# A queue written out unit by unit, global keys and values written in place, and four banks for the last outputs, in a fused attention and maxout kernel

## Chip, cores and metric

The kernel runs on one core of one Trainium2 chip. The metric is device time in microseconds (us) of one execution, as the median of several runs; before the change it is 216.99 us (216.52 to 217.34, three runs).

## What is computed

Attention over a band of 96 keys plus the first 8 keys of each batch, with a bias that falls with distance, then a feed-forward part that takes the maximum of three products:

```python
def _attn_ref(q, k, v, n_global, n_local):            # q, k, v: (4, 8, 768, 64) f32
    scores = scale * np.matmul(q, k.transpose(0, 1, 3, 2))
    rel = pos[:, None] - pos[None, :]
    is_global = pos[None, :] < 8
    is_local = (rel >= 0) & (rel < 96)
    dist = np.where(is_global & ~is_local, 96.0, np.abs(rel))
    slopes = 2.0 ** (-8.0 * (np.arange(H) + 1) / H)
    scores = scores - slopes[:, None, None] * dist
    scores = np.where(is_global | is_local, scores, -1e9)
    a = np.exp(scores - max);  a = a / (sum(a) + 1e-09)
    return np.matmul(a, v)

x = attention.transpose(0, 2, 1, 3).reshape(3072, 512)
h = np.maximum(np.maximum(x @ w1, x @ w2), x @ w3)    # w1..w3: (512, 768)
out = h @ w_out                                       # w_out: (768, 512)
```

## The kernel before

**Tiles.** The 4 batches of 768 rows are 24 tiles of 128 rows, T = 0 to 23, six to a batch. A row sees keys of its own tile, of the tile before, and the 8 global keys of its batch. So each tile has two blocks of scores, against itself and against the tile before, and the first 8 keys of the tile before are replaced by the global ones. The first tile of a batch has one block.

**Steps of a tile**, each a function. `load` issues three DMAs (q, k, v) on SP into one of 6 `raw` buffers. `cast` makes bf16 of q and k (line 115) and of v (line 117) on POOL. `u_X` (X) transposes q and k on PE, eight matmuls into the one `tp` bank, and ACT copies the result to `qkT` (line 148). `make_kg` and `make_vg` on POOL copy the transposed keys and the values to tiles of their own and put the global keys and values over the first 8 (lines 136 and 137, 125 and 126). `u_S` (S) makes the scores of four heads, and ACT their exponential (line 178); there are two groups of heads, g = 0 and 1, and one bank pair `sp`. DVE multiplies with the weights of mask and bias (M, line 182). `u_A` (A) multiplies with the values on PE; DVE divides by the sum. `u_XT` (XT) transposes the tile's result back on PE and DVE copies it to `xT`.

**Feed-forward.** Tiles are gathered to chunks of 4, 2, 2, 4, 4, 4 and 4. For chunk c, F1(c,f,j) is the product of xT with block f (0 to 5) of weight j (0 to 2): four matmuls, 512 columns wide for a chunk of four tiles and 256 for two. ACT copies j = 0, DVE takes the maximum with j = 1 and j = 2. F2(c,tt), the output of one tile, is six matmuls into the single `po` bank, a copy on ACT (line 249) and a DMA on SP. Weights come as nine DMAs, three to a group g = f // 2, and are cast by ACT, DVE and POOL (lines 273 to 275); w_out comes as three DMAs and is cast by ACT.

**Order.** No scheduler orders the instructions: each engine runs its own in the order in which the program issues them, and waits where data or a buffer is missing. The list `att` holds the attention steps; for chunk c the loop emits F1 units and the outputs of chunk c-1, and spreads the attention steps of chunk c+1 evenly between them. An M is emitted one step after its S. Casts, key and value copies and loads hang on X: X of tile T is followed by its copies, the cast of tile T+1 and the loads up to tile T+5. The three casts of a weight group go together, the first after the attention of chunk 0, the others after F1(0,0,2) and F1(0,2,2).

Of the kernel before, what the change touches and what calls it, by code (L numbers as in the profile page):

```python
# [19 lines left out]
def kernel(  # L20
# [13 lines left out]
    nc = tc.nc  # L34
# [28 lines left out]
    kg_pool = ctx.enter_context(tc.tile_pool(name="kg", bufs=3))  # L63
# [23 lines left out]
    vg_ring = [persist.tile([128, H * 65], BF16, name=f"vg{i}") for i in range(3)]  # L87
# [21 lines left out]

    def cast(T):  # L110
        b, t = divmod(T, NT)
        r = raw[T]
        qk = cast_pool.tile([128, 2, DM], BF16, name="qkb", tag="qkb")
        qb[T] = qk
        nc.gpsimd.tensor_copy(qk, r[:, 0:2].rearrange("p a h d -> p a (h d)"))  # L115
        va[T] = va_first[b % 2] if t == 0 else va_ring[T % NVA]
        nc.gpsimd.tensor_copy(heads(va[T])[:, :, 0:D], r[:, 2])  # L117

    def make_vg(T):
        b, t = divmod(T, NT)  # L120
        if t == 0:
            vg[T] = va[T]
        elif t < NT - 1:
            vg[T] = vg_ring[T % 3]
            nc.gpsimd.tensor_copy(words(vg[T]), words(va[T]))
            nc.gpsimd.tensor_copy(words(vg[T][0:NG]), words(va[b * NT][0:NG]))

    def make_kg(T):
        b, t = divmod(T, NT)
        kT = qkT[T][:, 1]  # L130
        if t == 0:
            kgT[T] = kT
            nc.gpsimd.tensor_copy(kg8[b % 2], kT[:, :, 0:NG])
        elif t < NT - 1:
            kgT[T] = kg_pool.tile([128, NP, 128], BF16, name="kgT", tag="kgT")
            nc.gpsimd.tensor_copy(words(kgT[T]), words(kT))  # L136
            nc.gpsimd.tensor_copy(kgT[T][:, :, 0:NG], kg8[b % 2])

    def u_X(T):
        if T < NSTART and T % 2:  # L140
# [8 lines left out]
        make_kg(T)  # L149
        make_vg(T)  # L150
        return []

    def u_S(T, g):
        b, t = divmod(T, NT)
        alt = T < NSTART and g == 1
# [25 lines left out]
        if t:  # L181
            return [lambda: nc.vector.tensor_mul(P, P, wmask[:, g])]  # L182
        return [lambda: nc.vector.tensor_mul(P[:, :, 0], P[:, :, 0], wmask0[:, g])]

    def u_A(T, g):
        b, t = divmod(T, NT)
        if T < NSTART and g == 1:
# [4 lines left out]
        for j2 in range(2):  # L192
            for hh in range(2):
# [5 lines left out]
                if t:  # L199
                    nc.tensor.matmul(o, P[:, i, 1], heads(vg[T - 1])[:, h], start=False, stop=True,  # L200
# [8 lines left out]
        return []  # L209

    def u_XT(T):
# [3 lines left out]
        tp = psT.tile([128, NP, 128], BF16, name="xtp", tag="tp")  # L215
# [4 lines left out]
        return []  # L220
# [4 lines left out]
    def u_F1(c, f, j):  # L225
# [15 lines left out]
        return []  # L241

    def u_F2(c, tt):
        po = psP.tile([128, DM], FP32, name="po", tag="po")
        for f in range(NF):
            nc.tensor.matmul(po, ht[c][:, f, tt * 128:(tt + 1) * 128], wo[:, f],  # L246
                             start=(f == 0), stop=(f == NF - 1))
        ost = ost_pool.tile([128, DM], FP32, name="ost", tag="ost")
        nc.scalar.copy(ost, po)  # L249
        T = chunks[c][tt]  # L250
        nc.sync.dma_start(out=out[T * 128:(T + 1) * 128, :], in_=ost)
        return []
# [5 lines left out]
    def load_w(g):  # L258
        for j in range(3):
            st = stage_pool.tile([128, 4, 256], FP32, name="wst", tag="wst")  # L260
            wst[g, j] = st
            nc.sync.dma_start(out=st, in_=wsrc[j][:, g * 256:(g + 1) * 256].rearrange(  # L262
                "(i p) f -> p i f", p=128))

    def load_wo():
        for i in range(3):
            st = stage_pool.tile([128, 2, DM], FP32, name="wst", tag="wst")
            wst["o", i] = st
            nc.sync.dma_start(out=st, in_=moe_w_out[i * 256:(i + 1) * 256, :].rearrange(
                "(i p) f -> p i f", p=128))  # L270

    def cast_w(g):
        nc.scalar.copy(w123[g][:, :, 0], wst[g, 0])
        nc.vector.tensor_copy(w123[g][:, :, 1], wst[g, 1])
        nc.gpsimd.tensor_copy(w123[g][:, :, 2], wst[g, 2])

    def cast_wo(i):
        nc.scalar.copy(wo[:, 2 * i:2 * i + 2], wst["o", i])

    with tc.manual_schedule():  # L280
# [36 lines left out]

        loads = [("T", T) for T in range(1, NSTART)] + [("w", 0), ("w", 1), ("T", NSTART),
                                                        ("w", 2), ("T", NSTART + 1), ("o",)]
        loads += [("T", T) for T in range(NSTART + 2, NTT)]  # L320
        done = [0]

        def upto(*what):
            if what[0] == "T" and what[1] >= NTT:
                return
            while what in loads[done[0]:]:
                x = loads[done[0]]
                done[0] += 1
                if x[0] == "T":
                    load(x[1])  # L330
                elif x[0] == "w":
                    load_w(x[1])
                else:
                    load_wo()


        att = []
        for i in range(NSTART):
            att.append(("X", i))
            if i >= 1:  # L340
                att += [("A", i - 1, 0), ("A", i - 1, 1)]
            att += [("S", i, 0), ("S", i, 1)]
            if i >= 1:
                att.append(("T", i - 1))
        i = NSTART - 1
        att += [("A", i, 0), ("X", i + 1), ("A", i, 1), ("S", i + 1, 0), ("T", i)]
        for i in range(NSTART, NTT + 1):
            if i < NTT and i > NSTART:
                att.append(("S", i, 0))
            if i > NSTART:  # L350
                att.append(("A", i - 1, 1))
            if i < NTT:
                att.append(("S", i, 1))
            if i + 1 < NTT:
                att.append(("X", i + 1))
            if i < NTT:
                att.append(("A", i, 0))
            if i > NSTART:
                att.append(("T", i - 1))
# [103 lines left out]
```

## Time and profile before

| | |
|---|---|
| median of 3 runs | 216.99 us |
| profiled execution | 216.65 us, its span 214.9 us |
| TensorE (PE) busy | 182.7 us, 85% |
| VectorE (DVE) busy | 121.5 us, 57% |
| ScalarE (ACT) busy | 113.0 us, 53% |
| GpSimd (POOL) busy | 66.1 us, 31% |
| read from HBM, written | 25.17 MB, 6.29 MB |

A timeline row gives the start in the span, the time an instruction took, its engine and line, and in brackets the idle time before it and what ended that. SPq is SP's queue, where DMAs are issued; an issue that takes long has waited for room in the DMA queue. A chain row names what held up the end of the program at that moment. PE's matmuls overlap, so the price of a unit is from its start to the next one's start.

### The profile page before, as it was taken

The numbers are of one execution on the slowest core, as the hardware profiler recorded it, in microseconds if no ns is written. First come the engines' busy times: TensorE is split into PE (matmuls) and PEld (weight loads), VectorE is DVE, ScalarE is ACT, GpSimd is POOL, SyncE is SP. The second block draws the span as 40 slices with busy tenths as digits, with TensorE's granted clock in tenths as the row PEclk, the third lists the DMA queues.
The fourth block names the chain that finished last, engine by engine and source line by source line (L and its number), as shares of the span: only waits on it lengthen the run. The fifth ranks groups of instructions, "written<-read, shape, count | busy, mean of one in ns | idle before, by whom it ended". The sixth has DMA issues, their size and how long they took to land.

```text
span 214.9 us, 4230 instructions
## 1 busy us (share of the span) xinstructions
PE 182.7 (85%) x1640; PEld 103.1 (48%) x1640; DVE 121.5 (57%) x266; ACT 113.0 (53%) x165; POOL 66.1 (31%) x131
## 2 busy tenths in 40 slices
PE   0446825998999999789999999999999999999962
PEld 0335622543566776466555455545544555444420
DVE  2164714576674648875876878565765666532400
ACT  5855504775765756566657635565564552233231
POOL 4654322437405047135433703135505000000000
PEclk9999999999999999999999999999999999999999
DMA  7999999999999894889547980111101111012122
GB/s 151 219 218 338 319 247 274 344 193 221 219 208 222 221 259 80 195 187 196 112 110 172 232 175 0 52 49 50 52 0 52 49 49 52 2 49 83 64 100 98
DMA packets 83924, 31.73 MB, mean 148 GB/s; under 512 B 75456, under 2 KB 80064, under 8 KB 83904
## 3 DMA queue, kind: packets, MB, share of 16 engines
q1 hardware_dynamic: 83904, 31.46, 64.1%
q8 instruction: 13, 0.21, 0.4%
q14 instruction: 7, 0.06, 0.1%
HBM read 25.17 MB, written 6.29 MB: 146 GB/s over the span
## 4 chain that ended last, share of the span: by engine, by line
PE 60%; SPq 17%; ACT 10%; DMA 4%; DVE 4%; issue 2%; POOL 1%; ACTq 0%
PE h L231 35%; PE po L246 14%; SPq L108 13%; ACT P L178 5%; DMA raw<-in_v_dram 4%; PE sp L168 4%; SPq L262 3%; DVE P L182 3%; PE xtp L218 2%; ACT qkT L148 2%; PE tp L146 2%; PE op L197 2%; ACT h L236 1%; ACT ost L249 1%; PE op L200 1%
## 5 line engine op out<-in xcount | busy, mean ns | idle before, releaser
L231 PE MATMUL h<-xT,w 128*128 128x512 bf16 (+1 forms) x504 | 110.7, 353 | 3.1 <-DVE xT L219 1.6
L231 PEld LDWEIGHTS <-w 128*128 128x128 bf16 x504 | 44.0, 98 | 35.9 <-issue 1.8
L178 ACT ACTIVATE P<-sp 128x1024 bf16<-128x1024 f32 (+1 forms) x44 | 42.1, 958 | 21.6 <-PE sp L168 21.6
L182 DVE TENSOR_TENSOR P<-P,wmask 128x1024 bf16<-128x1024 bf16 x40 | 33.6, 845 | 25.0 <-ACT P L178 24.6
L238 DVE TENSOR_TENSOR h<-h,h 128x512 bf16<-128x512 bf16 (+1 forms) x42 | 25.5, 608 | 29.0 <-PE h L231 28.4
L246 PE MATMUL po<-wo,ht 128*128 128x512 bf16 x144 | 35.0, 379 | 2.2 <-ACT ost L249 2.2
L236 ACT CAST h<-h 128x512 bf16<-128x512 f32 (+1 forms) x42 | 22.2, 528 | 22.5 <-PE h L231 22.2
L249 ACT COPY ost<-po 128x512 f32<-128x512 f32 x24 | 14.1, 586 | 37.2 <-PE po L246 34.1
L115 POOL CAST qkb<-raw 128x1024 bf16<-128x1024 f32 x24 | 24.8, 1034 | 15.7 <-DMA raw<-in_k_dram 15.7
L148 ACT COPY qkT<-tp 128x1024 bf16<-128x1024 bf16 x22 | 22.3, 1014 | 13.2 <-PE tp L146 13.2
L240 DVE TENSOR_TENSOR ht<-h,h 128x512 bf16<-128x512 bf16 (+1 forms) x42 | 25.5, 608 | 5.2 <-PE h L231 3.3
L146 PE MATMUL tp<-identb,qkb 128*128 128x128 bf16 x176 | 14.9, 234 | 13.6 <-POOL qkb L115 10.7
L136 POOL COPY kgT<-qkT 128x256 int32<-128x256 int32 x16 | 6.7, 416 | 59.7 <-ACT qkT L148 59.7
L146 PEld LDWEIGHTS <-qkb 128*128 128x128 bf16 x192 | 13.8, 108 | 19.8 <-POOL qkb L115 14.7
L246 PEld LDWEIGHTS <-ht 128*128 128x128 bf16 x144 | 13.2, 98 | 16.0 <-issue 3.0
L207 DVE TENSOR_TENSOR xb<-op,rz 128x256 bf16<-128x256 f32 x44 | 18.7, 424 | 1.5
L197 PEld LDWEIGHTS <-P 128*128 128x128 bf16 x192 | 15.0, 103 | 7.7 <-DVE xb L207 2.3
L168 PE MATMUL sp<-qkT 64*128 64x128 bf16 x204 | 14.1, 231 | 3.7 <-ACT qkT L148 2.9
L168 PEld LDWEIGHTS <-qkT 64*128 64x128 bf16 x224 | 7.6, 101 | 19.5 <-issue 15.7
L197 PE MATMUL op<-va,P 128*128 128x65 bf16 x148 | 14.6, 198 | 2.5 <-DVE xb L207 1.5
L200 PEld LDWEIGHTS <-P 128*128 128x128 bf16 x160 | 12.2, 103 | 2.4
L117 POOL CAST va<-raw 128x512 bf16<-128x512 f32 x20 | 12.7, 635 | 0.1
(52 smaller groups left out, 128.8 us busy)
## 6 DMA issues: line engine op xcount, KB each, us to landing
raw<-in_q_dram SPq DMA_DIRECT2D x24, 256.0 KB, 5.0
raw<-in_k_dram SPq DMA_DIRECT2D x24, 256.0 KB, 5.0
raw<-in_v_dram SPq DMA_DIRECT2D x24, 256.0 KB, 5.0
out_dram<-ost SPq DMA_DIRECT2D x24, 256.0 KB, 2.0
wst<-in_moe_w_dram SPq DMA_DIRECT2D x9, 512.0 KB, 6.5
wst<-in_moe_w_out_dram SPq DMA_DIRECT2D x3, 512.0 KB, 5.4
```

Source lines behind the costliest of these rows:

```text
L108: nc.sync.dma_start(out=r[:, i], in_=src[b, :, sl, :].rearrange("h s d -> s h d"))
L115: nc.gpsimd.tensor_copy(qk, r[:, 0:2].rearrange("p a h d -> p a (h d)"))
L146: nc.tensor.transpose(tp[:, a, jp], qb[T][:, a, jp * 128:(jp + 1) * 128], identb)
L148: nc.scalar.copy(qkT[T], tp)
L168: nc.tensor.matmul(sps[hh][:, j2, ds], st, qkT[T][hsl, 0, jp], start=True, stop=True, skip_group_check=True)
L178: nc.scalar.activation(P[:, :, 0:n], sp.rearrange("p a b d n -> p (a b) d n")[:, :, 0:n], AF.Exp, bias=0.0, scale=scale)
L182: return [lambda: nc.vector.tensor_mul(P, P, wmask[:, g])]
L197: nc.tensor.matmul(o, P[:, i, 0], heads(va[T])[:, h], start=True, stop=(t == 0), skip_group_check=True)
L231: nc.tensor.matmul(ps, w123[f // 2][:, dm, j, (f % 2) * 128:(f % 2) * 128 + 128], xT[c][:, dm], start=(dm == 0), stop=(dm == 3))
L238: nc.vector.tensor_max(h01s[c, f], h01s[c, f], ps)
L240: nc.vector.tensor_max(ht[c][:, f], h01s[c, f], ps)
L246: nc.tensor.matmul(po, ht[c][:, f, tt * 128:(tt + 1) * 128], wo[:, f], start=(f == 0), stop=(f == NF - 1))
```

## The change

A string, `SCHEDULE`, names every unit in the order in which it is issued; one loop calls the function of each. Letters are L load, w and o weight loads, C cast (`.0` for q and k, `.1` for v), X, S, M, A as above, T for XT, G for the global keys, V for the global values, F for F1, O for F2, W and Q casts of weights, E the last four outputs.

Beside the order, these things change. `make_kg` and `make_vg` are gone: G and V write the 8 global columns and rows into the tile itself, after its own S and A have read it, and S and A of the next tile read it there. The casts of q and k and of v are two units; for tiles 0 to 3, DVE casts q and POOL k. Each M, each weight load and each weight cast is a unit. All X use the bank `tp`, and XT of tiles 0 to 3 a bank of F1. The last four outputs have a bank each (`po`, `op`, `tp`, `sp`); two at a time get five of their six matmuls before the sixth; the copies of the last two are split between ACT and DVE.

```diff
+SCHEDULE = """
+    C0.0 X0 L1 S0.0 C1.0 M0.0 S0.1 G0 X1 C0.1 S1.0 S1.1 M0.1 L2 C2.0 X2 M1.0 C1.1 G1 M1.1 A0.0 L3 C3.0
...
+    A2.0 A2.1 M3.1 T1 G3 S4.0 w1.0 C3.1 w1.2 W0.0 L6 V2 w2.0 w2.1 C5.0 A3.0 A3.1 T2 M4.0 w2.2 L7 X5 S4.1
...
+"""
-    kg_pool = ctx.enter_context(tc.tile_pool(name="kg", bufs=3))
-    vg_ring = [persist.tile([128, H * 65], BF16, name=f"vg{i}") for i in range(3)]
-    def cast(T):
+    def cast(T, what):
         b, t = divmod(T, NT)
         r = raw[T]
+        if what == 1:
+            va[T] = va_first[b % 2] if t == 0 else va_ring[T % NVA]
+            nc.gpsimd.tensor_copy(heads(va[T])[:, :, 0:D], r[:, 2])
+            return
         qk = cast_pool.tile([128, 2, DM], BF16, name="qkb", tag="qkb")
         qb[T] = qk
-        nc.gpsimd.tensor_copy(qk, r[:, 0:2].rearrange("p a h d -> p a (h d)"))
-        va[T] = va_first[b % 2] if t == 0 else va_ring[T % NVA]
-        nc.gpsimd.tensor_copy(heads(va[T])[:, :, 0:D], r[:, 2])
-
-    def make_vg(T):
...
-            nc.gpsimd.tensor_copy(words(vg[T]), words(va[T]))
-            nc.gpsimd.tensor_copy(words(vg[T][0:NG]), words(va[b * NT][0:NG]))
-
-    def make_kg(T):
...
-            nc.gpsimd.tensor_copy(words(kgT[T]), words(kT))
-            nc.gpsimd.tensor_copy(kgT[T][:, :, 0:NG], kg8[b % 2])
+        flat = r.rearrange("p a h d -> p a (h d)")
+        if T < 4:
+            nc.vector.tensor_copy(qk[:, 0], flat[:, 0])
+            nc.gpsimd.tensor_copy(qk[:, 1], flat[:, 1])
+        else:
+            nc.gpsimd.tensor_copy(qk, flat[:, 0:2])
+
+    def put_kg(T):
+
+        b, t = divmod(T, NT)
+        kT = qkT[T][:, 1]
+        if t == 0:
+            nc.gpsimd.tensor_copy(kg8[b % 2], kT[:, :, 0:NG])
+        elif t < NT - 1:
+            nc.gpsimd.tensor_copy(kT[:, :, 0:NG], kg8[b % 2])
+
+    def put_vg(T):
+        b, t = divmod(T, NT)
+        if 0 < t < NT - 1:
+            nc.gpsimd.tensor_copy(words(va[T][0:NG]), words(va[b * NT][0:NG]))
...
-                    st = qkT[T][hsl, 1, jp] if ds == 0 else kgT[T - 1][hsl, jp]
+                    st = qkT[T][hsl, 1, jp] if ds == 0 else qkT[T - 1][hsl, 1, jp]
...
-                    nc.tensor.matmul(o, P[:, i, 1], heads(vg[T - 1])[:, h], start=False, stop=True,
+                    nc.tensor.matmul(o, P[:, i, 1], heads(va[T - 1])[:, h], start=False, stop=True,
...
+    last = NCH - 1
+    spare = ["po", "op", "tp", "sp"]
+
+    def f2_mm(c, tt, fs):
+        if (c, tt) not in pos_:
+            tag = spare[tt % 4] if c == last else "po"
+            pool = {"po": psP, "op": psO, "tp": psT, "sp": psS}[tag]
+            pos_[c, tt] = pool.tile([128, DM], FP32, name="po", tag=tag)
+        for f in fs:
+            nc.tensor.matmul(pos_[c, tt], ht[c][:, f, tt * 128:(tt + 1) * 128], wo[:, f],
+                             start=(f == 0), stop=(f == NF - 1))
+
+    def f2_out(c, tt):
+        po = pos_[c, tt]
+        T = chunks[c][tt]
+        ost = ost_pool.tile([128, DM], FP32, name="ost", tag="ost")
+        if T >= NTT - 2:
+            for i, copy in enumerate((nc.scalar.copy, nc.vector.tensor_copy)):
+                sl = slice(i * 256, (i + 1) * 256)
+                copy(ost[:, sl], po[:, sl])
+            nc.sync.dma_start(out=out[T * 128:(T + 1) * 128, :], in_=ost)
...
+    def cast_w(g, j):
+        copy = (nc.scalar.copy, nc.vector.tensor_copy, nc.gpsimd.tensor_copy)[j]
+        copy(w123[g][:, :, j], wst[g, j])
...
+    def u_E():
+        n = len(chunks[last])
+        for tt in range(0, n, 2):
+            two = range(tt, min(tt + 2, n))
+            for x in two:
+                f2_mm(last, x, range(NF - 1))
+            for x in two:
+                f2_mm(last, x, [NF - 1])
+                f2_out(last, x)
...
+        units = {"L": load, "w": load_w, "o": load_wo, "C": cast, "X": u_X, "S": u_S, "M": u_M,
+                 "A": u_A, "G": put_kg, "V": put_vg, "T": u_XT, "F": u_F1, "W": cast_w,
+                 "Q": cast_wo, "O": u_F2, "E": u_E}
+        for u in SCHEDULE.split():
+            units[u[0]](*(int(n) for n in u[1:].split(".") if n))
```

SP's queue at the start, before, from the second weight group on. `raw_220` and `raw_230` are tiles 4 and 5, `wst` the weights:

```order
L262 DMA wst_214<-in_moe_w1_dram 128x4x256
L262 DMA wst_216<-in_moe_w2_dram 128x4x256
L262 DMA wst_218<-in_moe_w3_dram 128x4x256
L108 DMA raw_220<-in_q_dram 128x8x64
L108 DMA raw_220<-in_k_dram 128x8x64
L108 DMA raw_220<-in_v_dram 128x8x64
L262 DMA wst_224<-in_moe_w1_dram 128x4x256
L262 DMA wst_226<-in_moe_w2_dram 128x4x256
L262 DMA wst_228<-in_moe_w3_dram 128x4x256
L108 DMA raw_230<-in_q_dram 128x8x64
L108 DMA raw_230<-in_k_dram 128x8x64
L108 DMA raw_230<-in_v_dram 128x8x64
```

Here tiles 0 to 3 and the first weight group are already ahead, and tiles 4 and 5 follow the second and the third group.

SP's queue at the same place, now. `raw_334` and `raw_470` are tiles 5 and 6:

```order
L142 DMA raw_334<-in_q_dram 128x8x64
L142 DMA raw_334<-in_k_dram 128x8x64
L142 DMA raw_334<-in_v_dram 128x8x64
L315 DMA wst_371<-in_moe_w1_dram 128x4x256
L315 DMA wst_373<-in_moe_w2_dram 128x4x256
L315 DMA wst_388<-in_moe_w3_dram 128x4x256
L315 DMA wst_390<-in_moe_w2_dram 128x4x256
L315 DMA wst_464<-in_moe_w1_dram 128x4x256
L315 DMA wst_467<-in_moe_w3_dram 128x4x256
L142 DMA raw_470<-in_q_dram 128x8x64
L142 DMA raw_470<-in_k_dram 128x8x64
L142 DMA raw_470<-in_v_dram 128x8x64
```

Tiles 4 and 5 now stand ahead of all weights, and tile 6 between the weights of group 1 and group 2.

POOL's queue around the first weight casts, before. `raw_230`, `raw_277` and `raw_350` are tiles 5, 6 and 7; `w123_0` and `w123_1` are weight groups:

```order
L125 COPY vg1_121<-va0_114 128x260
L126 COPY vg1_121<-vaf0_118 8x260
L115 CAST qkb_520<-raw_230 128x1024
L117 CAST va1_115<-raw_230 128x8x64
L275 CAST w123_0_125<-wst_212 128x4x256
L115 CAST qkb_597<-raw_277 128x1024
L117 CAST vaf1_119<-raw_277 128x8x64
L275 CAST w123_1_126<-wst_218 128x4x256
L133 COPY kg8_1_124<-qkT_697 128x32
L115 CAST qkb_700<-raw_350 128x1024
```

Each weight cast stands behind the casts of a whole tile, that of group 1 behind those of tile 6.

POOL's queue around the same casts, now. `raw_279`, `raw_330`, `raw_334` and `raw_470` are tiles 3, 4, 5 and 6:

```order
L149 CAST va3_114<-raw_279 128x8x64
L172 COPY va2_113<-vaf0_115 8x260
L158 CAST qkb_479<-raw_334 128x1024
L326 CAST w123_0_119<-wst_388 128x4x256
L149 CAST va0_111<-raw_330 128x8x64
L172 COPY va3_114<-vaf0_115 8x260
L167 COPY qkT_405<-kg8_0_117 128x4x8
L326 CAST w123_1_120<-wst_467 128x4x256
L158 CAST qkb_629<-raw_470 128x1024
L149 CAST va1_112<-raw_334 128x8x64
```

The cast of group 1 no longer stands behind that of tile 6, the v of a tile is cast later than its q and k, and the key and value copies stand apart from the casts of the next tile.

## Rows read from the trace of the kernel before

**Rows 1.** Timeline of POOL, casts of q and k: start, us, engine line, [idle before <-releaser].
```profile
9.01 1.04 POOL L115 CAST qkb<-raw 128x1024 bf16<-128x1024 f32 x1
...
29.68 1.04 POOL L115 CAST qkb<-raw 128x1024 bf16<-128x1024 f32 x1 [4.62 <-DMA raw<-in_k_dram]
...
37.64 1.04 POOL L115 CAST qkb<-raw 128x1024 bf16<-128x1024 f32 x1 [3.19 <-DMA raw<-in_k_dram]
...
45.31 1.04 POOL L115 CAST qkb<-raw 128x1024 bf16<-128x1024 f32 x1 [5.03 <-DMA raw<-in_k_dram]
...
49.97 1.04 POOL L115 CAST qkb<-raw 128x1024 bf16<-128x1024 f32 x1 [0.57 <-DMA raw<-in_k_dram]
```
**Rows 2.** Chain of waits, 38 to 50 us: start, us, what the end waited on.
```profile
38.79 8.79 DMA raw<-in_v_dram
...
48.26 0.99 POOL w L275
...
49.30 1.04 PE h L231 x4
```
**Rows 3.** Windows: stretch, us; busy us (instructions) of PE, PEld, DVE, ACT, POOL; PEclk, DMA, GB/s.
```profile
75.00:107.00 32.00, 28.75 (x340) 19.33 (x338) 23.32 (x55) 19.49 (x28) 13.62 (x28) 1.00 0.83 173
107.00:151.00 44.00, 43.24 (x410) 22.72 (x409) 30.06 (x63) 25.79 (x34) 15.95 (x31) 1.00 0.47 103
151.00:203.00 52.00, 52.00 (x364) 25.52 (x362) 28.28 (x55) 21.42 (x31) 5.94 (x12) 1.00 0.12 46
```
**Rows 4.** Chain of waits, the last four outputs.
```profile
203.24 1.31 PE po L246 x6
...
208.96 0.59 ACT ost L249
...
209.59 1.47 PE po L246 x6
```
**Rows 5.** Chain of waits, stretches of PE alone: start to start is a unit's price.
```profile
72.63 0.44 PE h L231 x4
73.06 0.45 PE tp L146 x8
...
106.10 0.33 PE sp L168 x8
106.43 0.97 PE h L231 x4
107.40 0.03 PE op L197
...
107.64 1.29 PE po L246 x6
...
111.79 0.22 PE xtp L218 x4
...
179.93 7.77 PE h L231 x36
```
**Rows 6.** Timeline of SP, issues of v of tiles 1 and 2.
```profile
5.00 1.18 SPq L108 DMA_DIRECT2D raw<-in_v_dram  x1
...
8.55 1.10 SPq L108 DMA_DIRECT2D raw<-in_v_dram  x1
```
**Rows 7.** Timeline of PE, first and third F1 unit.
```profile
35.75 1.86 PE L231 MATMUL h<-xT,w 128*128 128x512 bf16 x4 [1.64 <-DVE xT L219]
...
40.42 1.03 PE L231 MATMUL h<-xT,w 128*128 128x512 bf16 x4
```
**Rows 8.** Timelines of DVE and POOL, 84 to 87 us.
```profile
84.19 2.87 DVE L182 TENSOR_TENSOR P<-P,wmask 128x1024 bf16<-128x1024 bf16 x1
...
85.91 0.61 POOL L117 CAST vaf<-raw 128x512 bf16<-128x512 f32 x1
```
**Rows 9.** The line of the full multiplies: duration ns min/median/max, first and last start.
```profile
L182 DVE TENSOR_TENSOR P<-P,wmask x40: 677/691/2872, 14.0 to 176.3; 128x1024 bf16<-128x1024 bf16 x40
```
**Rows 10.** Groups by line and shape: the exponentials; busy, mean ns, idle before.
```profile
L178 ACT ACTIVATE P<-sp 128x1024 bf16<-128x1024 f32 x37 | 38.0, 1026 | 17.3 <-PE sp L168 17.2
```

More of the change, by code (lines that the diff above doesn't have):

```diff
@@ L90 @@
     wo = persist.tile([128, NF, DM], BF16, name="wo")
-    raw, qb, kb, qkT, kgT, Pt, ops, xb, rzs = {}, {}, {}, {}, {}, {}, {}, {}, {}
+    raw, qb, qkT, Pt, xb = {}, {}, {}, {}, {}
     xT = {}
-    va, vg = {}, {}
+    va = {}
     def words(ap):
@@ L148, in u_X @@
         nc.scalar.copy(qkT[T], tp)
-        make_kg(T)
-        make_vg(T)
-        return []
     def u_S(T, g):
         b, t = divmod(T, NT)
-        alt = T < NSTART and g == 1
+        alt = early(T) and g == 1
         if alt:
@@ L180, in u_S, with u_M @@
                                  AF.Exp, bias=0.0, scale=scale)
-        if t:
-            return [lambda: nc.vector.tensor_mul(P, P, wmask[:, g])]
-        return [lambda: nc.vector.tensor_mul(P[:, :, 0], P[:, :, 0], wmask0[:, g])]
+    def u_M(T, g):
+        P = Pt[T, g]
+        if T % NT:
+            nc.vector.tensor_mul(P, P, wmask[:, g])
+        else:
+            nc.vector.tensor_mul(P[:, :, 0], P[:, :, 0], wmask0[:, g])
     def u_A(T, g):
         b, t = divmod(T, NT)
-        if T < NSTART and g == 1:
+        if early(T) and g == 1:
             op = psP.tile([128, 4, 65], FP32, name="opp", tag="po")
@@ L214, in u_XT @@
             xT[c] = xT_pool.tile([128, NP, len(chunks[c]) * 128], BF16, name="xT", tag="xT")
-        tp = psT.tile([128, NP, 128], BF16, name="xtp", tag="tp")
+        where_xt = 'h2' if early(T) else 'tp'
+        pool = {'h2': psH, 'tp': psT, 'po': psP, 'op': psO}[where_xt]
+        tp = pool.tile([128, NP, 128], BF16, name="xtp", tag=where_xt)
         x = xb[T].rearrange("p h d -> p (h d)")
@@ L219, in u_XT @@
         nc.vector.tensor_copy(xT[c][:, :, i * 128:(i + 1) * 128], tp)
-        return []
     ht = {}
@@ L240, in u_F1 @@
             nc.vector.tensor_max(ht[c][:, f], h01s[c, f], ps)
-        return []
-    def u_F2(c, tt):
[L244 to L252, printed above, removed]
+    pos_ = {}
@@ new lines @@
+    last = NCH - 1
[17 more added lines that the diff above has]
+            nc.sync.dma_start(out=out[T * 128:(T + 1) * 128, :], in_=ost)
+        else:
+            nc.scalar.copy(ost, po)
+            nc.sync.dma_start(out=out[T * 128:(T + 1) * 128, :], in_=ost)
@@ L254 @@
+    def u_F2(c, tt):
+        f2_mm(c, tt, range(NF))
+        f2_out(c, tt)
     wsrc = [moe_w1, moe_w2, moe_w3]
     wst = {}
[L258 to L275, printed above, removed]
+    def load_w(g, j):
+        st = stage_pool.tile([128, 4, 256], FP32, name="wst", tag="wst")
+        wst[g, j] = st
+        nc.sync.dma_start(out=st, in_=wsrc[j][:, g * 256:(g + 1) * 256].rearrange(
+            "(i p) f -> p i f", p=128))
+    def load_wo(i):
+        st = stage_pool.tile([128, 2, DM], FP32, name="wst", tag="wst")
+        wst["o", i] = st
+        nc.sync.dma_start(out=st, in_=moe_w_out[i * 256:(i + 1) * 256, :].rearrange(
+            "(i p) f -> p i f", p=128))
@@ L315 @@
                                  scale=-slopes[h])
[L318 to L334, printed above, removed]
@@ L337 @@
[L337 to L359, printed above, removed]
```

101 lines of the change are left out of this document (27 added, 74 removed).

## Prediction

> **What bounds the kernel now.** I read the windows table first, for the time in which TensorE (PE) stands idle; then the chain of waits, for what each stage waited on; then the timelines of GpSimd (POOL), SyncE (SP) and PE for the start. They show three regimes.
>
> To 49.3 us the loads set the pace. Casts of q and k start the moment k lands, at 29.68, 37.64, 45.31 and 49.97 us for tiles 4 to 7 [rows 1], and the chain into the third weight unit of chunk 0's second group, F1(0,2,2), is a load, a POOL queue and a weight cast: that cast waits in POOL's queue behind the casts of tile 6, whose v lands at 47.6, and ends at 49.25; the unit starts at 49.30 [rows 2]. The weight itself had been issued long before tile 6.
>
> From 49.3 to 203.2 us PE sets the pace. Between 151 and 203 us PE is busy all 52.00 us, between 107 and 151 it is idle 0.76, between 75 and 107 it is idle 3.25 [rows 3]. From 203.24 us on PE and ScalarE (ACT) take turns: each of the last four outputs starts when the copy before it has emptied the one bank, and the units last 1.47 instead of 1.29 [rows 4, 5].
>
> So I count **PE work that is left**. Prices from start to start at full rate: a 512-column F1 unit 7.77/9 = 0.863, a 256-column one 0.44, an output (F2) 1.29, a tile's eight transposes (X) 0.45, a back transpose (XT) 0.22, a score group (S) 0.33 plus the 0.11 by which the next F1 unit is longer = 0.44, a value group (A) 0.24; half of the last two for the first tile of a batch, which has one block instead of two [rows 5]. All of it is 170.5 us, and the change takes none away.
>
> Before, from F1(0,2,2) at 49.30 on there are 82 units of 0.863, 36 of 0.44, 24 of 1.29, 17 X, 20 XT, 30 full and 6 half S, 31 full and 6 half A: 152.3 us, so PE could be done at 201.6. The last four outputs begin at 203.24 with 5.2 left [rows 4]: they would end at 208.4, so 6.8 us were lost in the middle; they end at 211.06, so 2.6 were lost there. From the end of the last matmul, 209.59 + 1.47, to the end of the span are 3.84 us [rows 4].
>
> **The start: order of loads and of first units.** All DMA of the kernel stands in SP's queue. Before: tiles 0 to 3, six weights, tile 4, three weights, tile 5, three of w_out, tiles 6, 7. Now: tiles 0 to 5, six weights, tile 6, three weights, tile 7, w_out, tile 8. Nothing is added, so the queue is as full and only landing times change. A tile takes 3.55 to 3.70 us of the queue, say 3.65 [rows 6]; six weights take 29.68 - 9.01 - 3 x 3.65 = 9.7, so 1.62 each (9.01 is the start of tile 1's cast and not surely its landing: an error of half a us either way); w_out takes 45.31 - 37.64 - 3.65 = 4.0 [rows 1].
>
> New landings: q and k of tile 5 at 9.0 + 4 x 3.65 = 23.6, its v at 24.8; the first three weights at 26.4, 28.0, 29.7; tile 7's q and k w_out earlier than before, 49.97 - 4.0 = 46.0; the ninth weight just ahead of tile 7, at 43.6; tile 8, with the same bytes ahead of it as before, one tile after tile 7 of before, 53.6. Each cast costs 1.04 [rows 1]. PE then has these earliest ends, start plus work left:
> - F1(0,0,2) after the third weight's cast: 30.75, with 159.5 left: 190.3.
> - F1(0,4,2) after the ninth's: 44.65, 146.2 left: 190.9.
> - X of tile 8: 53.6 + 1.04 = 54.65, 135.7 left: 190.4.
>
> These lines meet, so one hidden behind another gives little. The first units come after idle time and run at 1.2 GHz: before, the first took 1.86, the third 1.03 [rows 7]. Two such units fit before 30.75 (start at 26.4 + 1.04 = 27.45, then about 1.75 each); a third would add 0.8. I take 191.0, bounds 190.3 to 192. Against 201.6 that is 10.6 us gained, the largest term. The split cast (q of tiles 0 to 3 on VectorE (DVE), k on POOL) and the use of one bank for early X cost nothing I can find: tiles arrive 3.65 apart, and a cast split in two can save at most half of 1.04 on the first. The cover is the load; without it four casts would stand in DVE's queue ahead of the first multiplies, each at most as long as POOL's 1.04.
>
> **The middle: own places for multiplies, casts and key copies.** POOL loses 16 full key copies and 16 full value copies, all of them beside PE's work. In their place eight key columns (G) and eight value rows (V) are written into the tile itself. G(T) now waits until S(T) has been read, V(T) until A(T) has; behind them in POOL's queue stand casts of later tiles, and S(T+1) and A(T+1) wait for them. From tile 7 on PE has at least 1.5 us of other units between S(T) and S(T+1), and 1.5 between A(T) and A(T+1); an 8-wide copy with its handover is under 0.5. Price nothing, unless a cast of 1.04 is ahead, and then still near nothing.
>
> The multiplies M are worth more: one took 2.87, from 84.19 to 87.06, where the median of the 40 full ones is 0.69, and in that time POOL ran casts one behind the other until 86.52 [rows 8, 9]. The Trainium skill, "SBUF — State Buffer", section "SBUF: two separate sides", says that DVE with two SBUF inputs and GpSimd hold their shared ports by an exclusive lock, for one whole instruction. By that an M would wait for one cast, 1.04 here, and shorter casts would do more good; the row has it waiting for more than one, so a run of casts is what counts, and the sum keeps to the row.
>
> Does the middle lose less than 6.8? For: fewer POOL instructions, each M placed by itself, tiles 8 to 23 spread until just before chunk 6. Against: where 14.5 us of PE work stand, from F1(1,0,0) to the third output of chunk 0, ACT has, up to the second output's copy, 4 exponentials of 1.03 [rows 10], three weight casts and two copies of transposes of about that length, and seven shorter copies: about 12 us in 12.6 of PE. I take 4.0, bounds 0.8 (what 107 to 151 shows as idle) and 9.0 (6.8 and one more M of 2.2 too long).
>
> **The end.** The last four outputs go to four banks, and two at a time get five matmuls each before their sixth: no wait for a copy, 2.6 us gained. The last copies are split over ACT and DVE, 0.59 to some 0.4, but two transfers are issued close together. The second issue costs between nothing and 1.18, as a load's does on a full queue [rows 6]; this queue is all but empty, so 0.3: 3.9 after the last matmul, bounds 3.7 to 4.8. This end does not collide with loads, which are over.
>
> **Sum.** 191.0 + 4.0 + 3.9 = 198.9 us of span. The profiled execution took 216.65 for a span of 214.9, so 1.75 lie around it: 200.65. The median, 216.99, stands 0.3 above that execution: **201.0 us**. In terms: 10.6 at the start, 2.8 in the middle, 2.6 at the end, all three less time.
>
> **Rivals.**
> 1. *The middle loses as much as before or more* (chance 0.14). ACT is full for 12 us, and casts in a row, like those of tiles 21, 22, 19 behind one another, hold M back as at 84.19. Stalls of 6.8 to 9: 203.8 to 206.
> 2. *PE stays at 1.2 GHz through chunk 0* (0.06). The new order starts F1 while weights still land, with gaps. Before, the third unit already ran at 1.03 with waits ahead of it [rows 7], which speaks against. If ten more units each cost 1.86 - 1.03 = 0.83 more, 8.3 on the first line: about 209. The Trainium skill, "TensorE: Matmul & The Clock Gate", section "HAM oscillation — how this bites in real kernels", tells of such kernels, in which each wait for a load sends the array back to the lower rate.
> 3. *The in-place writes become the bound* (0.05; slower). POOL is one queue in order: if G(T) and V(T) are each reached behind a q/k cast and a v cast, a tile waits up to 2 x 1.65 more. 16 tiles have both; at half of it, 1.65 a tile, 26 us: 227. It turns the result over from (217 - 201)/16 = 1.0 us a tile. Against: the 1.5 us of cover above; and PE hardly waits from 107 us on though POOL has the same casts there [rows 3].
> 4. *The planned queue fits badly as a whole and the gain is spent in many small waits* (0.02, no change): 10.6 + 2.6 lost again over 24 tiles, 0.7 a tile.
>
> **How the numbers follow.** Forecast 0.73, 196.9 to 203.5: the low end is 190.3 + 0.8 + 3.7 + 1.75 + 0.3 = 196.9. The range goes up to 192 + 9.0 + 4.8 + 1.75 + 0.3 = 207.8 and takes in rival 1. 0.5% is about what a measurement of this kernel can tell from no change; faster by more than that: 0.73 + 0.14 + 0.06 = 0.93, the same 0.02, slower 0.05.
>
> **What would show it.** Right: the first F1 unit near 27.5 us and F1(0,4,2) near 44.7; X of tile 8 near 54.7; four outputs at the end with no wait of PE for an ACT copy, 5.2 us in all; idle PE after 60 us about 2 to 4 us, where an M is long or ACT is full. Wrong: weights that land later than 30 us for the third; first units of 1.8 beyond the third; PE waiting for G or V in the list of waits; more than 7 us lost between X of tile 8 and the last four outputs.

## The result, and the profile after

The changed kernel takes **202.25 us** (201.14 to 203.52, four runs) against 217.0: a ratio of 0.932 (0.926 to 0.938). Another four runs of it, beside the experiments, gave 202.07 (201.27 to 202.64). The forecast was 201.0, and three terms of time saved. All three are there, each off by some: in the profiled execution the start saves 7.9 us instead of 10.6, the middle 3.4 instead of 2.8, the end 1.9 instead of 2.6. In a second profiled execution of the same kernel, the first under Experiments, the start saves 9.3.

The profiled execution is the slowest of its four, 203.52 us with a span of 201.7. The windows answer to [rows 3]: PE's idle time between 75 and 107 us, 3.25 before, is gone, and what is left stands between 107 and 151.

```profile
75.00:107.00 32.00, 31.99 (x354) 20.51 (x353) 24.49 (x57) 21.08 (x29) 12.12 (x20) 1.00 0.96 208
107.00:151.00 44.00, 42.10 (x385) 21.66 (x383) 32.16 (x61) 25.66 (x33) 12.29 (x22) 1.00 0.42 96
151.00:189.00 38.00, 38.00 (x249) 18.72 (x248) 19.62 (x39) 13.27 (x21) 0.79 (x2) 1.00 0.13 49
```

The chain of waits at the start is short now: k of tile 8 is issued at 47.67 us, lands after 8.79, is cast by POOL and transposed by PE. From there PE sets the pace. Before, the chain went through a weight cast behind tile 6 [rows 2].

```profile
47.67 8.79 DMA raw<-in_k_dram
...
56.93 1.05 POOL qkb L158
...
58.03 0.62 PE tp L181 x8
```

POOL's timeline shows the casts by which the start was worked out: the third and the ninth weight, q/k of tiles 7 and 8 (start, us, line, idle before and what ended it).

```profile
31.45 1.04 POOL L326 CAST w<-wst 128x1024 bf16<-128x1024 f32 x1 [5.60 <-DMA wst<-in_moe_w_dram]
...
45.05 1.04 POOL L326 CAST w<-wst 128x1024 bf16<-128x1024 f32 x1 [4.28 <-DMA wst<-in_moe_w_dram]
...
47.25 1.04 POOL L158 CAST qkb<-raw 128x1024 bf16<-128x1024 f32 x1 [1.17 <-DMA raw<-in_k_dram]
...
56.93 1.04 POOL L158 CAST qkb<-raw 128x1024 bf16<-128x1024 f32 x1 [1.43 <-DMA raw<-in_k_dram]
```

PE's timeline, first six F1 units and the last four outputs. The last four now run without a wait; in [rows 4] each waited for a copy.

```profile
29.44 7.20 PE L267 MATMUL h<-xT,w 128*128 128x512 bf16 x24 [1.42 <-ACT w L326]
...
191.78 5.34 PE L288 MATMUL po<-wo,ht 128*128 128x512 bf16 x24
```

With the method of the prediction, start plus work left: X of tile 8 gives 58.03 + 135.7 = 193.7. The last matmul ends at 191.78 + 5.34 = 197.1, so 3.4 us are lost between. From there to the end of the span are 4.6.

The 3.4 have one large piece, in the timelines of DVE and POOL. A multiply M, 0.69 us in the median before [rows 9], took 4.09 at 116.53. POOL started a run of casts at the same moment and ended it at 118.06 + 2.02 = 120.08; M ended 0.54 after that. The M of 2.87 before ended 0.54 after its run of casts too [rows 8].

```profile
116.53 4.09 DVE L217 TENSOR_TENSOR P<-P,wmask 128x1024 bf16<-128x1024 bf16 x1
...
116.52 1.03 POOL L158 CAST qkb<-raw 128x1024 bf16<-128x1024 f32 x1
117.50 0.61 POOL L149 CAST vaf<-raw 128x512 bf16<-128x512 f32 x1
118.06 2.02 POOL L158 CAST qkb<-raw 128x1024 bf16<-128x1024 f32 x2
```

At the end, the timelines of ACT, DVE and SP: each of the last two outputs is copied in two halves, and DVE's half waits for ACT's half of the same output.

```profile
196.99 0.65 ACT L298 COPY ost<-po 128x256 f32<-128x256 f32 x2 [1.52 <-issue]
...
197.39 0.76 DVE L298 COPY ost<-po 128x256 f32<-128x256 f32 x2 [4.72 <-ACT ost L298]
...
197.84 0.81 SPq L299 DMA_DIRECT2D out_dram<-ost  x2
```

### The profile page after: what moved, and what is told of

Its sections match the earlier page's. It is cut to its first block, busy times and chain, and to the rows that moved or that the text cites. A ratio compares the mean times of both kernels' runs of the same rounds, so it can differ in the third digit from the quotient of the medians.

```text
span 201.7 us, 4239 instructions
## 1 busy us (share of the span) xinstructions
PE 180.7 (90%) x1640; PEld 103.0 (51%) x1640; DVE 125.4 (62%) x272; ACT 113.0 (56%) x165; POOL 54.7 (27%) x99
## 4 chain that ended last, share of the span: by engine, by line
PE 61%; SPq 22%; DVE 7%; DMA 4%; issue 3%; POOL 1%; DVEq 0%; ACT 0%; POOLq 0%
PE h L267 33%; SPq L142 17%; PE po L288 15%; PE sp L200 4%; DMA raw<-in_k_dram 4%; SPq L315 4%; DVE P L217 4%; PE tp L181 3%; PE op L233 2%; PE xtp L255 2%; PE op L236 1%; DVE h L274 1%; SPq L321 1%; DVE ht L276 1%; POOL qkb L158 1%
## 5 line engine op out<-in xcount | busy, mean ns | idle before, releaser
L267 PE MATMUL h<-xT,w 128*128 128x512 bf16 (+1 forms) x504 | 106.5, 353 | 1.5 <-ACT w L326 1.4
L267 PEld LDWEIGHTS <-w 128*128 128x128 bf16 x504 | 46.0, 98 | 39.7 <-issue 2.0
L183 ACT COPY qkT<-tp 128x1024 bf16<-128x1024 bf16 x24 | 24.3, 1011 | 11.4 <-PE tp L181 10.4
L181 PE MATMUL tp<-identb,qkb 128*128 128x128 bf16 x192 | 17.5, 238 | 9.4 <-DVE qkb L155 4.5
L158 POOL CAST qkb<-raw 128x1024 bf16<-128x1024 f32 x20 | 20.9, 1047 | 15.9 <-DMA raw<-in_k_dram 11.9
L200 PE MATMUL sp<-qkT 64*128 64x128 bf16 x324 | 17.8, 230 | 3.6 <-ACT qkT L183 3.6
L200 PEld LDWEIGHTS <-qkT 64*128 64x128 bf16 x352 | 11.0, 101 | 13.9 <-issue 6.3
L233 PEld LDWEIGHTS <-P 128*128 128x128 bf16 x192 | 14.6, 102 | 4.7 <-DVE P L217 1.3
L172 POOL COPY va<-vaf 8x260 int32<-8x260 int32 x16 | 6.8, 422 | 29.3 <-PE op L236 29.3
L167 POOL COPY qkT<-kg 128x32 bf16<-128x32 bf16 x16 | 3.8, 236 | 37.3 <-PE sp L200 37.0
```

Source lines behind the costliest of these rows:

```text
L158: nc.gpsimd.tensor_copy(qk, flat[:, 0:2])
L200: nc.tensor.matmul(sps[hh][:, j2, ds], st, qkT[T][hsl, 0, jp], start=True, stop=True, skip_group_check=True)
L233: nc.tensor.matmul(o, P[:, i, 0], heads(va[T])[:, h], start=True, stop=(t == 0), skip_group_check=True)
L267: nc.tensor.matmul(ps, w123[f // 2][:, dm, j, (f % 2) * 128:(f % 2) * 128 + 128], xT[c][:, dm], start=(dm == 0), stop=(dm == 3))
```

## Experiments

**The changed kernel once more**, as the measure for the others.

> The changed kernel once more, on the chip of the next three, as their base. Both theories: 201 to 203.5 us. In its profile: the first F1 unit near 29 us, X of tile 8 near 57 to 58, a multiply of over 3 us near 116 with four casts of POOL beside it, and some 4 to 5 us from the last matmul to the end.

It gave 202.07 us, ratio 0.931. Its trace shows how much the start varies between executions of one kernel: tile 8's cast starts at 55.52 instead of 56.93, its transposes at 56.62 instead of 58.03, and the span is 200.2 instead of 201.7. Its first F1 units ran at full clock, those of the other execution mostly at 1.2 GHz; more of that under The start and the end.

```profile
55.52 1.04 POOL L158 CAST qkb<-raw 128x1024 bf16<-128x1024 f32 x1 [1.45 <-DMA raw<-in_k_dram]
```

### Which part brings what

**Loads alone**, in the kernel before:

```diff
-        loads = [("T", T) for T in range(1, NSTART)] + [("w", 0), ("w", 1), ("T", NSTART),
-                                                        ("w", 2), ("T", NSTART + 1), ("o",)]
-        loads += [("T", T) for T in range(NSTART + 2, NTT)]
+        loads = [("T", T) for T in range(1, NSTART + 2)] + [("w", 0), ("w", 1), ("T", NSTART + 2),
+                                                            ("w", 2), ("T", NSTART + 3), ("o",)]
+        loads += [("T", T) for T in range(NSTART + 4, NTT)]
```

> The kernel before, with its loads in the new order (tiles 4 and 5 ahead of the first six weights, tile 6 ahead of the last three, tile 7 ahead of w_out) and all else as it was, so that weight casts still stand behind whole tiles' casts. Theory (the order of the loads is the larger half of the start's gain, since tiles then arrive before they are asked for): F1(0,2,2) near 42 us instead of 49.3, 209 to 213 us. Rival (only the order of the units gives it; loads alone move the wait from tiles to weights): 215.5 us or more.

It gave 213.9 us (213.85 to 215.49), ratio 0.988 (0.985 to 0.990): 3.1 us of 15. That lies a little above the 209 to 213 of the theory, and F1(0,2,2) starts at 48.15 in the profiled execution (the slowest of the four), where the theory had 42 and the kernel before 49.30: the order of the loads alone is not the larger half of the start's gain. The data are early, but POOL does not get to them. Its timeline shows the cast of tile 5 at 31.91, behind the key and value copies of the tile before, for which POOL had waited 3.71 us on ACT; so the first F1 unit starts at 35.42, where it was 35.75 before [rows 7].

```profile
30.48 0.40 POOL L136 COPY kgT<-qkT 128x256 int32<-128x256 int32 x1 [3.71 <-ACT qkT L148]
...
31.91 1.03 POOL L115 CAST qkb<-raw 128x1024 bf16<-128x1024 f32 x1
...
35.42 1.87 PE L231 MATMUL h<-xT,w 128*128 128x512 bf16 x4 [3.79 <-DVE xT L219]
```

**Order of units, without the order of loads**: the changed kernel with the load order of before.

```diff
-    C0.0 X0 L1 S0.0 C1.0 M0.0 S0.1 G0 X1 C0.1 S1.0 S1.1 M0.1 L2 C2.0 X2 M1.0 C1.1 G1 M1.1 A0.0 L3 C3.0
+    C0.0 X0 L1 L2 L3 w0.0 w0.1 w0.2 w1.0 w1.1 w1.2 L4 w2.0 w2.1 w2.2 L5 o0 o1 o2 S0.0 C1.0 M0.0 S0.1
...
```

> The new kernel with one thing put back: the order in which SP issues its loads, as it was before (tiles 1 to 3, then all weights, then tiles 4 and 5). The queue of each engine keeps the new order of units. Theory (the order of units and the order of loads are worth their 10 us only together): X of tile 5 stands ahead of the first F1 unit in PE's queue, and tile 5's q/k landed at 37.6 us with the old loads, so F1(0,0,0) starts near 39.3 us instead of 29.4; with 161.2 us of PE work left, 3.4 lost in the middle, 4.7 after the last matmul and 1.75 outside the span that gives about 210 us, 207 to 212. Rival (the order of units brings the gain alone, loads only follow): 205 us or less.

It gave 215.46 us (214.99 to 215.75), ratio 0.992 (0.989 to 0.995). The direction was the theory's, the size was not: 215.5 against 207 to 212. PE waits 11.8 us for the q/k of tile 4 and 3.6 for tile 5, and the first F1 unit starts at 41.95, later than in the kernel before. The theory had it at 39.3, the landing and a cast; but the transposes of tile 5 begin only at 39.32, and scores, a back transpose and its copy stand between them and F1. That is 2.65 of the miss. The row of PE's wait list (us, times, longest), and the timelines of POOL and PE:

```profile
PE tp L182 <- POOL qkb L159: 15.4, 2, 11.8
```

```profile
38.23 1.04 POOL L159 CAST qkb<-raw 128x1024 bf16<-128x1024 f32 x1 [4.30 <-DMA raw<-in_k_dram]
...
39.32 1.03 PE L182 MATMUL tp<-identb,qkb 128*128 128x128 bf16 x8 [3.63 <-POOL qkb L159]
...
41.95 0.59 PE L268 MATMUL h<-xT,w 128*128 128x512 bf16 x1 [0.52 <-DVE xT L257]
```

The rest of it is lost behind: 41.95 + 161.2 = 203.15, the last matmul ends at 209.06, so 5.9 instead of 3.4. An M of 4.09 beside casts is again among it.

**Tail alone**, in the kernel before: the new functions for the outputs and nothing else.

```diff
+            tag = spare[tt % 4] if c == last else "po"
...
+        u_E()
```

> The kernel before, with the four banks and split copies for its last outputs and nothing else. Theory (2.6 us of waits go, and 0.9 come back between last matmul and end, since the two halves of a copy run one after the other): 215.2 to 215.8 us. Rival (the whole 2.6 stays, as predicted): 214.4 us.

It gave 215.09 us (215.02 to 215.37), ratio 0.991 (0.989 to 0.993): 1.9 us, a little more than the theory's range and short of the rival's 2.6.

**Everything but the tail**: the changed kernel with one bank for the last outputs.

```diff
-            tag = spare[tt % 4] if c == last else "po"
+            tag = "po"
...
-        if T >= NTT - 2:
+        if False:
```

> The changed kernel with its last four outputs as before: one bank, one after the other, one copy on ACT each. Theory (the end is worth 2.6 in waits, less what the two close transfers take back, some 0.9): slower by 1.5 to 2.5 us. Rival (the end is bound by the output transfers, so the banks give nothing): within 0.5 us.

It gave 203.23 us (202.6 to 204.66), ratio 0.939 (0.935 to 0.943), 13.8 us below the kernel before and 1.0 to 1.2 above the changed one, less than the 1.5 to 2.5 expected. In the trace the last four outputs take 189.03 to 197.01, 8.0 us where the change takes 5.34, and the span ends 3.8 us later where the change needs 4.6: 2.6 saved, 0.8 given back, 1.8 net. In this execution tile 8's transposes start at 55.46, 2.6 and 1.2 earlier than in the two of the change, so its span hides a part of that; whether its other three runs start as early, and so why the medians differ by less, is not shown. The first and the last of the four outputs, on PE:

```profile
189.03 1.46 PE L289 MATMUL po<-wo,ht 128*128 128x512 bf16 x6
...
195.55 1.46 PE L289 MATMUL po<-wo,ht 128*128 128x512 bf16 x6 [0.72 <-ACT ost L302]
```

So loads alone bring 3.1, the order of units with the tail 1.6, the tail alone 1.9, and loads with the order of units 13.8. The split of the first q and k casts and the use of one bank for all X are part of the order of units here; they were not tried alone. **The order of loads and the order of units are worth their gain only together.** What is called early must also be reached early in the queues of POOL and PE, and the other way round.

**Global keys and values copied whole, as before, within the new order**, each copy right behind its X or its cast of v, and with six value tiles instead of three.

```diff
-            nc.gpsimd.tensor_copy(kT[:, :, 0:NG], kg8[b % 2])
+            kgT[T] = kg_pool.tile([128, NP, 128], BF16, name="kgT", tag="kgT")
+            nc.gpsimd.tensor_copy(words(kgT[T]), words(kT))
+            nc.gpsimd.tensor_copy(kgT[T][:, :, 0:NG], kg8[b % 2])
...
+            vg[T] = vg_ring[T % 6]
+            nc.gpsimd.tensor_copy(words(vg[T]), words(va[T]))
```

> The changed kernel with whole copies of keys and values on POOL again, now with six value tiles; q and k casts stand where they stood. Theory (in-place writes carry little of the gain): 202 to 204 us, with some more multiplies of over 1.2 us. Rival (without the copies' removal the middle doesn't shrink): 206 us or more, and the multiplies' line busy for 40 us or more instead of 33.6.

It gave 201.7 us (201.38 to 203.09), ratio 0.931 (0.928 to 0.934): no difference. POOL is busy 69.5 us instead of 54.7, and the time is none the longer. Writing the global parts in place brings none of the gain by itself, given the six value tiles. A first form of this kernel, with the three value tiles of the kernel before, took 212.22 us (211.68 to 212.71). In its order V17 overwrites the tile that A15.1 still has to read, so it computes something else, and its time is no price of the copies.

### What the middle loses

**The casts elsewhere.** In two kernels the casts of tiles 18 to 20 were called at other places: first those of 19 and 20 and the v of 18 ahead of V16; then earlier still, in two pairs, as shown.

```diff
-    A15.1 M16.0 C17.0 F3.5.0 X17 L19 L20 L21 L22 V15 F3.5.1 A16.0 F3.5.2 G16 S17.0 T15 M16.1 O2.1 F4.0.0
-    F4.0.1 M17.0 A16.1 C18.0 X18 F4.0.2 V16 S17.1 M17.1 F4.1.0 F4.1.1 C19.0 S18.0 C18.1 C20.0 T16 A17.0
+    F3.4.0 C17.1 F3.4.1 T14 L18 F3.4.2 S16.1 A15.1 M16.0 C17.0 F3.5.0 X17 L19 L20 L21 L22 C18.0 C19.0
+    V15 F3.5.1 A16.0 F3.5.2 G16 S17.0 T15 M16.1 O2.1 F4.0.0 F4.0.1 C18.1 C20.0 M17.0 A16.1 X18 F4.0.2
```

> The changed kernel with three casts (q and k of tiles 19 and 20, v of tile 18) queued on POOL before the value write of tile 16 instead of behind it; nothing else moves. Theory (the multiply of 4.1 us at 116 waits out four casts in a row, and PE loses 2 to 3 us by it): that multiply under 1.8 us, idle PE between 107 and 151 under 1 us instead of 1.9, and 1.5 to 3 us less time. Rival (the multiply waits for something else, or the loss is made up later by slack): the multiply stays above 3 us, or the time stays within 0.5 us.

> The changed kernel with the run of casts broken up in another way than in the run before: q and k of tiles 18 and 19 ahead of the value write of tile 15, v of tile 18 and q, k of tile 20 ahead of the second multiply pair of tile 17. Theory (a multiply waits out every cast that follows the last without a gap; 2.5 us of PE are lost between the second output of chunk 2 and the first of chunk 3): the longest multiply there under 2 us, work left plus start at the first output of chunk 3 no more than 1 us above that at the last of chunk 2, and 1.5 to 2.5 us less than the changed kernel's 202.1. Rival (that loss is made up by slack later): within 0.5 us of it.

They gave 202.39 us (201.83 to 204.03) and 202.08 us (200.89 to 203.03): no difference. In both the long M is still there, 3.72 us, at another place. In the profiled execution of the first PE stood 2.59 us for it, and PE's granted clock was 0.50 (1.2 GHz) from 113.2 to 116.4, after that wait; 5.8 us are lost there between X of tile 8 and the last outputs. The timelines of DVE and POOL of the second:

```profile
104.99 3.72 DVE L218 TENSOR_TENSOR P<-P,wmask 128x1024 bf16<-128x1024 bf16 x1
...
105.16 3.00 POOL L159 CAST qkb<-raw 128x1024 bf16<-128x1024 f32 x3
```

POOL still had three q/k casts in a row, and M ended 0.55 after them (108.71 against 108.16). To call casts at another place does not take the row apart, as POOL does them one behind another as soon as it reaches them with data and buffers there. This theory of mine, that the place alone mattered, fell.

**Two of the casts on ACT** instead:

```diff
-            nc.gpsimd.tensor_copy(qk, flat[:, 0:2])
+            (nc.scalar.copy if T in (19, 20) else nc.gpsimd.tensor_copy)(qk, flat[:, 0:2])
```

> The new kernel with the q/k casts of tiles 19 and 20 on ACT instead of POOL; nothing else is changed. They are two of the casts that stand in a row on POOL near 104 to 118 us, beside which one multiply M took 3.6 to 4.1 us and PE lost 2.5 us. Theory (M waits out the row of casts, because it and they work on the same SBUF, and PE follows M): the longest M there falls below 2 us, the line of PE start plus work left rises by under 1 us between O2.1 and O3.0, and the time is 199.6 to 200.6 us, 1.5 to 2.5 below the 202.1 of the new kernel. Rival (the 2.5 us are made up by another wait as soon as this one is gone, since ACT's exps come later by two casts of about 1 us): within 0.5 us of the new kernel.

It gave **200.85 us** (200.67 to 200.9), ratio 0.925 (0.922 to 0.927), 1.2 us below the 202.07 of the change. The longest M is 2.12 instead of 4.09, and it ends 0.55 after the shorter run of casts beside it (117.81 against 117.26).

```profile
115.69 2.12 DVE L217 TENSOR_TENSOR P<-P,wmask 128x1024 bf16<-128x1024 bf16 x1
...
115.67 0.61 POOL L149 CAST vaf<-raw 128x512 bf16<-128x512 f32 x1
116.23 1.03 POOL L158 CAST qkb<-raw 128x1024 bf16<-128x1024 f32 x1
...
57.36 0.62 PE L181 MATMUL tp<-identb,qkb 128*128 128x128 bf16 x8 [0.54 <-POOL qkb L158]
...
189.24 5.34 PE L288 MATMUL po<-wo,ht 128*128 128x512 bf16 x23
```

From X of tile 8 to the first of the last four outputs are 131.9 us here and 133.75 in the change; without any loss it would be 130.5. So the middle's loss goes from 3.25 to 1.4; in the second execution of the change it is 3.2. The theory's own sign is the line of start plus work left at the second output of chunk 2 and at the first of chunk 3, with 81.6 and 71.8 us of work left. In the chain of the change these two start at

```profile
112.80 1.29 PE po L288 x6
...
125.05 1.40 PE po L288 x6
```

so the line rises from 194.4 to 196.85, by 2.45. Here they start at

```profile
111.95 1.29 PE po L288 x6
...
122.23 1.40 PE po L288 x6
```

so it rises from 193.55 to 194.0, by 0.5, where under 1 was expected. The mechanism holds. The size was a little off: M did not fall below 2, and the gain is 1.2 where 1.5 to 2.5 stood.

### The start and the end

**PE kept busy ahead of the first F1 units** by eight matmuls whose results nobody uses, put before T2, T3 and F1(0,0,0):

```diff
+        def u_D(n):
+            d = psH.tile([128, 4, 128], FP32, name="h1", tag="h1")
+            for _ in range(n):
+                nc.tensor.matmul(d, identb, wmask[:, 0, :, 0, :], start=True, stop=True,
+                                 skip_group_check=True)
```

> The new kernel with some matmuls added whose results nobody uses, in the gaps of PE between 24 and 29 us ahead of the first F1 unit, so that PE is busier before it. Question: the first six F1 units took 7.2 us at a granted clock of 0.50, some 3 us more than at full clock. Theory (PE runs into X of tile 8 anyway, which waits for that tile's q/k to land and be cast at 55 to 58 us, so the clock of the start is not what sets the end): the first six F1 units may come down to 5 us or less, and the time stays within 0.7 us of the new kernel. Rival (the clock of the start sets the end): 1.5 us or more faster.

It gave 201.67 us (201.06 to 202.57), 0.4 below the change and inside its runs. Windows of the change and of this kernel, 27 to 34 us: the granted clock is 0.56 in the one (1.2 GHz for most of the stretch) and 1.00 in the other.

```profile
27.00:34.00 7.00, 5.58 (x25) 2.24 (x22) 2.02 (x4) 3.47 (x4) 2.09 (x4) 0.56 1.10 352
```

```profile
27.00:34.00 7.00, 6.18 (x36) 2.77 (x32) 3.58 (x7) 4.06 (x6) 2.09 (x4) 1.00 1.11 341
```

Of the same kernel, the timelines of PE and POOL:

```profile
31.09 3.63 PE L268 MATMUL h<-xT,w 128*128 128x512 bf16 x16 [0.77 <-POOL w L327]
...
55.21 1.04 POOL L159 CAST qkb<-raw 128x1024 bf16<-128x1024 f32 x1 [1.48 <-DMA raw<-in_k_dram]
```

That the added matmuls raised the clock is not shown. The second execution of the unchanged change also has 1.00 from 27 to 34 us, and its PE timeline is nearly the same:

```profile
31.49 3.63 PE L267 MATMUL h<-xT,w 128*128 128x512 bf16 x16 [0.84 <-POOL w L326]
...
56.62 0.62 PE L181 MATMUL tp<-identb,qkb 128*128 128x128 bf16 x8 [0.71 <-POOL qkb L158]
```

In both the units run at full speed, 3.63 for four; but PE then waits for a weight, 0.77 and 0.84, and in the end for tile 8, whose cast starts when its k has landed. In the first execution of the change, where the first six units took 1.9 us more than their price (the expectation has some 3), PE waited for tile 8 all the same:

```profile
58.03 0.62 PE L181 MATMUL tp<-identb,qkb 128*128 128x128 bf16 x8 [0.69 <-POOL qkb L158]
```

So the lower clock at the start did not set the end there; what it would cost with an early tile 8 no trace shows.

**The last two outputs copied whole**, one by ACT and one by DVE, together with the two casts on ACT:

```diff
-            for i, copy in enumerate((nc.scalar.copy, nc.vector.tensor_copy)):
-                sl = slice(i * 256, (i + 1) * 256)
-                copy(ost[:, sl], po[:, sl])
+            (nc.scalar.copy if T % 2 == 0 else nc.vector.tensor_copy)(ost, po)
```

> As the kernel with two q/k casts on ACT, and the last two outputs are copied out of PSUM whole, the one by ACT and the other by DVE, instead of each in two halves of which DVE's waited for ACT's (0.65 us, then 0.76 us). Theory (the halves of one tile run one after the other, so splitting them buys nothing): from the last matmul to the end of the span 4.2 to 4.5 us instead of 4.74, so 0.2 to 0.5 us less than the kernel with two q/k casts on ACT alone. Rival (the halves make the end shorter): 0.3 us or more slower than that kernel.

It gave **199.56 us** (199.07 to 200.35), ratio 0.919 (0.917 to 0.921), the fastest of all, 1.3 us below the one before it. The trace gives the tail only a small part of that: the last matmul ends at 194.15 and the span at 198.5, so 4.35 against 4.5. DVE's copy no longer waits for ACT's.

```profile
188.81 5.34 PE L288 MATMUL po<-wo,ht 128*128 128x512 bf16 x23
...
194.02 0.58 ACT L296 COPY ost<-po 128x512 f32<-128x512 f32 x1 [1.52 <-issue]
...
194.19 0.69 DVE L296 COPY ost<-po 128x512 f32<-128x512 f32 x1 [4.49 <-PE po L288]
```

So the edit is worth about 0.2 us at its own place, the lower end of what was expected. The two profiled executions are only 0.6 apart (198.5 and 199.1), and X of tile 8 starts 0.8 earlier in the one than in the other (56.59, 57.36), at a place that the edit doesn't touch. Where the rest of the 1.3 between the medians comes from is not settled.

## Why the prediction was right, step by step

- **The start** (largest term, 10.6 forecast): right in kind, 2.7 us too large in the profiled execution (base 193.7 instead of 191.0) and 1.3 in the second (56.62 + 135.7 = 192.3); both are outside the bounds of 190.3 to 192. The step that failed is "tile 8, with the same bytes ahead of it as before, ... 53.6". With the old order that was right: before, k of tile 8 was issued at 48.49, the row below, and by the same trace landed 4.9 us later, at 53.4. Now it is issued earlier, at 47.67, and lands 8.79 later, at 56.5; in the second execution at 55.1. So the same bytes took 1.7 to 3.1 us longer. A part had gathered before it: the third weight was 1.75 late, the ninth 1.45, tile 7 1.25. In the eleven traces with the new order of loads k of tile 8 landed between 52.7 and 56.5, in the three with the old one between 53.4 and 53.8. Why the new order spreads it so, no run takes apart.

```profile
48.49 1.03 SPq L108 DMA_DIRECT2D raw<-in_k_dram  x1
```

- **"These lines meet"** was off with it. The first F1 unit was 2.0 late: 29.44 + 161.2 = 190.6. With the 1.9 us that the first six took beyond their price (29.44 to 36.48 for 5.2) that is 192.5, and tile 8's line at 193.7 covers it.
- **The middle** (4.0 forecast, bounds 0.8 to 9.0): 3.4. The mechanism named, casts in a row that hold an M, is confirmed: 2.5 of the 3.4 are lost around the M of 4.09, and with two casts on ACT the loss falls to 1.4. Of the reasons given for less loss, fewer POOL instructions was not one: whole copies on POOL cost nothing. The M are no shorter than before (mean 849 ns against 845); whether their places, or the spread of tiles 8 to 23, lowered the loss from 6.8 to 3.4 no run takes apart.
- **In-place writes at no price**: right. The wait list of PE names no G and no V, and whole copies give the same time.
- **The end**: four outputs in 5.34, as forecast (5.2). Behind the last matmul 4.6 instead of 3.9, near the upper bound. The step "split over ACT and DVE, 0.59 to some 0.4" failed: DVE's half of a tile waited for ACT's, and with whole copies the end is 0.2 shorter.
- **The sum**: 193.7 + 3.4 + 4.6 = 201.7 instead of 198.9. In the second execution it is 192.3 + 3.3 + 4.6 = 200.2. The median is 1.3 below the first one and not 0.3 above it, and the middle lost less than forecast; so the time came out only 1.25 above the forecast. That it lies so near is in part luck: the largest term was outside its bounds.
- **The rivals**: the lower clock appeared in one of the two profiled executions, for about six units where ten more than two had been priced, and off the path. The middle lost less than before, not more. A new bound on POOL did not come up. That the plan fits badly was the case where half of it was undone: with the loads of before 215.5.

The Trainium skill, "SBUF — State Buffer", section "SBUF: two separate sides", has an exclusive lock between DVE and GpSimd for one whole instruction. The traces agree that M and POOL's casts hold each other up, but they show two lengths of it. In the rows above M waited for all that was left of a run, up to four casts, and ended 0.54 to 0.55 after the last of them. In the change, at 38.43, it ended some 0.5 after the one cast under way, and the next cast took 1.07 instead of 0.61:

```profile
38.43 1.52 DVE L217 TENSOR_TENSOR P<-P,wmask 128x1024 bf16<-128x1024 bf16 x1
...
38.23 1.19 POOL L158 CAST qkb<-raw 128x1024 bf16<-128x1024 f32 x1 [1.13 <-DMA raw<-in_k_dram]
39.36 1.07 POOL L149 CAST va<-raw 128x512 bf16<-128x512 f32 x1
```

What decides whether M gets its turn between two casts, no run shows.

## What to carry to other kernels

Count the work left on the bounding engine at each place where it could be held up; the latest of start plus work left is the end, and a gain at any other place is lost. Change the order of loads and the order in which each engine reaches the data together: either alone brought 3.1 us or less, both 13.8. Where a vector multiply shows several times its median, look for a run of casts on GpSimd beside it, and try to give some of them to another engine; moving them within the same queue did nothing here.

## What the runs showed of the hardware that I had not expected

- A multiply on DVE with two SBUF operands can wait out a whole run of POOL casts: 4.09, 3.72 and 2.12 us, each ending 0.54 to 0.55 after the run. It does not always: the one of 1.52 us got its turn after one cast.
- Of two halves of one output tile, copied by ACT and DVE from one PSUM bank into one SBUF tile, DVE's was released by ACT's. Whole tiles in two banks overlapped, from 194.02 and 194.19 on. Whether the program's tracking of the tile or of the bank made the half wait was not tried.
- The same kernel's load of tile 8 landed 1.4 us apart in two executions, at 56.5 and 55.1, and the spans were 1.5 apart. With the old order of loads it landed at 53.4, though it was issued later.
